# A decode kernel on one core: P V of loads 0 to 12 with 32 columns of P standing and V moving

## The chip, the core and the metric

The kernel runs on one core of a Trainium2 chip. A core has a matrix engine (PE), a vector engine (DVE), a scalar engine (ACT), a general engine (POOL), a queue engine (SP) that here issues almost all transfers, and sixteen DMA engines that carry them. [...] The metric is device time in microseconds (us) of one launch, median over runs.

A matmul has a stationary operand, which is loaded into the array first (LDWEIGHTS, "PEld" in the profile), and a moving operand, which is streamed through it. "Column groups" are matmuls whose stationary operand has 32 columns: each uses one quarter of the array and writes 32 partitions of PSUM, and four of them can be in flight side by side.

## The reference

One decode step of a transformer block for eight sequences: attention over the last 2048 cached positions with 32 query heads in 8 groups of 4, then an MLP whose token-mixing half vanishes for a sequence of length one.

```python
h = x + _A_ref(_layernorm(x), k_cache, v_cache, wq, wo)
out = h + _B_ref(_layernorm(h), w1, w2, w3, w4)
# _A_ref: B, D = 8, 512; Hq, Hkv, Dh = 32, 8, 128; W = 2048
q = (x @ wq) split into heads
scores = einsum("bhqd,bhkd->bhqk", q, k[last W]) * Dh**-0.5
p = softmax(scores); o = einsum("bhqk,bhkd->bhqd", p, v[last W])
return o @ wo
# _B_ref for S = 1: x1 = x (the shifted branch is zero); x1 + gelu(layernorm(x1) @ w3) @ w4
```

The caches are bfloat16. Of each, 8 x 8 x 2048 x 128 values are read, 33.5 MB.

## The kernel before

**Loads.** The caches are read in sixteen loads of 2 MB each for K and V. Load n belongs to sequence b = n // 2 and to half t = n % 2 of the eight groups (J = 4 groups). A partition holds 64 consecutive positions of one group: 32 partitions per group, four groups side by side. `load_k`, `load_v` and `load_wo` only issue transfers on SP's queue, in program order; a load waits there until its buffer is free (four buffers for K, four for V). `load_v(n)` waits for the last P V of load n − 4. The last load of V is cut into four pieces. All of wo, w3 and w4 follow at the end, but for two pieces of wo that are issued during loads 5 and 9.

**Engines.** Every engine has a list of operations (`PE.op`, `AC.op`, `DV.op`, `PO.op`), written in the order of the emission loop at the end of the function; each engine runs its list strictly in order, and an operation waits for the semaphore counts named in it. So the position of a call in the loop sets where an engine may stall.

**K.** `turn_K(i)` turns a quarter of a load, read as 32-bit words, with eight float32 transposes by PE (L296), into one of two PSUM tiles; ACT evicts the lower half (L283), DVE the upper (L284). `pe_QK(m)` multiplies with column groups of 32: a stationary 32-column window of `qz`, in which the four query columns stand at a place that depends on half and chunk, so that scores land in the right PSUM rows (L311). One PSUM tile `S_ps` holds the scores of a whole sequence.

**Softmax.** `softmax_1` to `softmax_3` take the row maximum (DVE L321), turn it (PE L325), reduce and negate it (DVE L327, L332), turn it back (PE L336) and take the exponential with its sum (ACT L342). In the next load `softmax_spread` writes P four times wider, P times a 0/1 mask over the four groups, in four parts of 512 columns (DVE L355); `softmax_4` turns this tile with sixteen bfloat16 transposes (PE L364), evicted through the same `turn` helper; `softmax_5` spreads the reciprocal of the sums (PE L372, DVE L375, L381).

**P V.** `pe_PV(i)` handles a quarter of a load: sixteen chunks of 128 positions, each one matmul with the chunk of V standing (128 columns) and 16 columns of the turned P moving (L397). All 64 matmuls of a load add up in the 16 columns `oT_ps[:, 0:16]`. `scale` (DVE L407) multiplies with the reciprocals, `turn_o` (PE L417, DVE L422) brings the result into the layout for wo.

**Order.** In iteration n of the loop K of load n is turned and scored and P V of load n − 3 is done (n − 4 in the last two iterations). The quarters of P V stand between the pieces of the score and softmax work (`pvs(1)` to `pvs(4)`); `turn_os` catches up with the out-turns near the start of an iteration. After the loop come, in this order, the spread of the last sequence, P V of load 12, softmax_5 and softmax_4, P V of loads 13 to 15 with half of wo in between (`pe_wo`), the rest of wo, and the MLP (L559 to L619).

Of the kernel before, what the change touches and what calls it, by code (L numbers as in the profile page):

```python
# [6 lines left out]
dt = mybir.dt  # L7
# [35 lines left out]
QW = 12 + R + 28  # L43
# [33 lines left out]
def bass_sequential_preLN__sliding_block_cached__mixer_s_mlp__decode_kernel(  # L77
# [24 lines left out]
    with es:  # L102
# [15 lines left out]
        perm_p = sb([128, 128], dt.bfloat16, "perm_p")  # L118
# [35 lines left out]
        oK = sb([128, 2, J, R, R], dt.bfloat16, "oK")  # L154
        o2 = sb([128, G, R, B], dt.bfloat16, "o2")
# [34 lines left out]
        def dma(eng, dst, src, sem, *waits):  # L190
            def f(e):
# [25 lines left out]
        e_sel = DV.op(lambda e: e.tensor_reduce(sel_f[:, :].rearrange("p (j h) -> p j h", j=J),  # L217
                                                ident_f[:, :].rearrange("p (j u h) -> p j h u", j=J, u=U),
                                                AX.X, ALU.add), e_idf)
        e_mE = DV.op(lambda e: e.tensor_reduce(mE[:, :], ident_f[:, :].rearrange("p (e k) -> p e k", k=R),  # L220
# [44 lines left out]
        def fill_q(b):  # L265
            for c in range(2):
                at = 12 + 16 * c
# [34 lines left out]
        def pe_QK(m):  # L302
            n, v = divmod(m, 2)
            b, t = divmod(n, NU)
            lo = 12 - 8 * v - 4 * t
# [18 lines left out]
        def softmax_2(b):  # L324
            e_mT[b] = PE.op(lambda e: e.matmul(sm[0:1, MROW], mcol[:, :], ident_f[:, :], start=True, stop=True),  # L325
                            e_max[b], sm_read[0], e_idf)
            e = DV.op(lambda e: e.tensor_reduce(Mrow[:, :].rearrange("o (j h) -> o j h", j=J),  # L327
                                                sm[0:1, MROW].rearrange("o (j u h) -> o j h u", j=J, u=U),
                                                AX.X, ALU.max), e_mT[b])
            sm_read[0] = e  # L330
            m_bc = bass.AP(tensor=Mrow[:, :].tensor, offset=0, ap=[[H, 1], [8, J], [0, U], [1, 8]])
            e_neg[b] = DV.op(lambda e: e.tensor_scalar(negrow[:, :].rearrange("o (j u h) -> o j u h", j=J, u=U), m_bc,  # L332
# [13 lines left out]
        def softmax_spread(b, part):  # L346
            if part == 0:
# [3 lines left out]
            p = P_sb[:, w * part:w * part + w]  # L351
            p_bc = bass.AP(tensor=p.tensor, offset=p.offset, ap=[p.ap[0], [1, w], [0, J]])
            m = mJ[:, :]
            m_bc = bass.AP(tensor=m.tensor, offset=m.offset, ap=[m.ap[0], [0, w], [1, J]])
            e_Pz[b, part] = DV.op(lambda e: e.tensor_tensor(  # L355
                Pz[:, 0, J * w * part:J * w * (part + 1)].rearrange("p (x j) -> p x j", j=J), p_bc, m_bc, ALU.mult),
                e_exp[b], e_PT.get(b - 1), e_mJ)

        def softmax_4(b):
            s = b % 2  # L360

            def mm(e, ps, half):
                for c in range(8 * half, 8 * half + 8):
                    ins = e.matmul(ps[:, c * 128:(c + 1) * 128], Pz[:, 0, c * 128:(c + 1) * 128], perm_p[:, :],  # L364
                                   is_transpose=True)
                return ins
# [20 lines left out]

        def pe_PV(i):
            n, w = divmod(i, U)
            b, t = divmod(n, NU)  # L390
            dst = oT_ps[:, 0:16]

            def f(e):
                for c in range(16):
                    o = (8 * (w % 2) + c // 2) * 128 + 16 * (2 * (2 * (c % 2) + w // 2) + t)
                    mvg = pS[:, b % 2, o:o + 16]
                    ins = e.matmul(dst, vnat[:, n % NV, (16 * w + c) * DH:(16 * w + c + 1) * DH], mvg,  # L397
                                   start=(w == 0 and c == 0), stop=(w == U - 1 and c == 15),
                                   skip_group_check=True)
                return ins  # L400
            e_PV[i] = PE.op(f, V(n, w), *e_pS[b], e_sc.get(n - 1))

        def scale(n):
            b, t = divmod(n, NU)
            src = oT_ps[:, 0:16]
# [3 lines left out]
                            e_rL[b], e_PV[U * n + U - 1], e_scale.get(n - 2))  # L409
# [54 lines left out]
        def emit_PV(i):  # L464
            if i % U == 1 and i > U:
                turn_os(i // U)
                if i // U == NUN - 1:
                    pe_wo((0, 1, 2, 3), e_scale[NUN - NU], (sem_wo, 16 * len(WO_AT)))
            pe_PV(i)
            if i % U == U - 1:  # L470
                scale(i // U)
# [184 lines left out]
```

## Time and profile before

| | |
|---|---|
| median of three runs | 197.41 us (197.41 to 197.92) |
| the profiled execution | 197.34 us, span 196.0 us |
| busy, PE / PEld / DVE / ACT / POOL | 153.8 / 125.9 / 98.2 / 85.9 / 7.0 us |
| DMA | 79.52 MB, mean 406 GB/s |
| mean granted clock of PE | 0.872 |
| P V on PE (L397) | 1024 matmuls, 33.2 us busy |
| turn of K on PE (L296) | 512 transposes, 76.1 us busy |
| turn of P on PE (L364) | 128 transposes, 9.4 us busy |
| spread of P on DVE (L355) | 32 instructions, 21.6 us busy |

How to read it: the span runs from the first to the last instruction of the profiled execution. Busy times of different engines overlap, and matmuls overlap one another, so they don't add up to the span. An arrow names what an engine waited for; "issue" means that the profile shows nothing that it waited for. The granted clock is 1.0 or 0.5 at any moment; 0.872 is its mean. The slices of the page are a fortieth of the span each, 4.9 us. Instructions of an engine are themselves brought by DMA, in queues of their own (q8 and q14 on the page).

### The profile page before, as it was taken

The numbers are of one execution on the slowest core, as the hardware profiler recorded it, in microseconds if no ns is written. First come the engines' busy times: TensorE is split into PE (matmuls) and PEld (weight loads), VectorE is DVE, ScalarE is ACT, GpSimd is POOL, SyncE is SP. The second block draws the span as 40 slices with busy tenths as digits, with TensorE's granted clock in tenths as the row PEclk, the third lists the DMA queues.
The fourth block names the chain that finished last, engine by engine and source line by source line (L and its number), as shares of the span: only waits on it lengthen the run. The fifth ranks groups of instructions, "written<-read, shape, count | busy, mean of one in ns | idle before, by whom it ended". The sixth has DMA issues, their size and how long they took to land.

```text
span 196.0 us, 5301 instructions
## 1 busy us (share of the span) xinstructions
PE 153.8 (78%) x2415; PEld 125.9 (64%) x2415; DVE 98.2 (50%) x223; ACT 85.9 (44%) x100; POOL 7.0 (4%) x28
## 2 busy tenths in 40 slices
PE   0038985978989898989885789898989897888464
PEld 0037852765869577868773668586958585777453
DVE  5302444865484566548553384549455765620130
ACT  6001565764456374735471355535635482230030
POOL 4001001001000100010001000100000000000000
PEclk9999999999699999997999579969997999555555
DMA  6999999999999999999999999999999999999970
GB/s 229 461 408 431 425 431 431 421 428 425 423 420 422 431 425 428 423 425 428 419 427 421 431 428 425 428 425 428 425 428 421 423 421 428 407 405 407 406 285 24
DMA packets 7542, 79.52 MB, mean 406 GB/s; under 512 B 856, under 2 KB 864, under 8 KB 3424
## 3 DMA queue, kind: packets, MB, share of 16 engines
q1 hardware_dynamic: 7504, 79.18, 96.1%
q8 instruction: 19, 0.31, 0.6%
q14 instruction: 3, 0.02, 0.0%
q10 hardware_dynamic: 16, 0.01, 0.0%
HBM read 79.18 MB, written 0.01 MB: 404 GB/s over the span
## 4 chain that ended last, share of the span: by engine, by line
DMA 51%; PE 31%; DVE 10%; SPq 5%; issue 2%
DMA knat<-in_A_k_cache_dram 42%; PE kT_ps L296 21%; DMA knat<-in_B_w_dram 9%; SPq L192 5%; PE S_ps L311 5%; DVE kT_sb L284 5%; DVE Pz L355 2%; PE kT_ps L364 2%; DVE mcol L321 1%; PE oT_ps L397 1%; PE sm L325 1%; PE sm L336 1%; DVE Mrow L327 1%; PE S_ps L607 1%; DVE negrow L332 0%
## 5 line engine op out<-in xcount | busy, mean ns | idle before, releaser
L283 ACT ACTIVATE kT_sb<-kT_ps 128x1024 bf16<-128x1024 bf16 x64 | 63.8, 1024 | 47.2 <-PE kT_ps L296 46.5
L296 PE MATMUL kT_ps<-perm_k,knat 128*128 128x128 f32 x512 | 76.1, 306 | 3.4 <-DMA knat<-in_A_k_cache_dram 3.2
L296 PEld LDWEIGHTS kT_ps<-perm_k,knat 128*128 128x128 f32 x512 | 65.7, 159 | 9.1 <-issue 4.3
L284 DVE TENSOR_SCALAR kT_sb<-kT_ps 128x512 int32<-128x512 int32 x64 | 44.2, 690 | 35.0 <-PE kT_ps L296 34.8
L397 PEld LDWEIGHTS oT_ps<-pS,vnat 128*128 128x128 bf16 x1024 | 30.5, 98 | 6.4 <-issue 6.1
L397 PE MATMUL oT_ps<-pS,vnat 128*128 128x16 bf16 x1024 | 33.2, 171 | 1.3 <-DVE oK L407 1.3
L311 PE MATMUL S_ps<-kT_sb,qz 128*32 128x512 bf16 x256 | 20.0, 386 | 11.0 <-DVE kT_sb L284 10.6
L355 DVE TENSOR_TENSOR Pz<-P_sb,mJ 128x512 bf16<-128x512 bf16 x32 | 21.6, 684 | 0.0
L342 ACT ACTIVATE P_sb<-S_ps,negcol 128x512 bf16<-128x512 f32 x8 | 5.5, 688 | 24.9 <-DVE negcol L339 24.9
L283 ACT ACTIVATE pS<-kT_ps 128x1024 bf16<-128x1024 bf16 x8 | 8.2, 1024 | 15.8 <-PE kT_ps L364 15.8
L311 PEld LDWEIGHTS S_ps<-kT_sb,qz 128*32 128x32 bf16 x256 | 4.7, 94 | 15.8 <-ACT kT_sb L283 14.8
L284 DVE TENSOR_SCALAR pS<-kT_ps 128x512 int32<-128x512 int32 x8 | 5.5, 692 | 9.4 <-PE kT_ps L364 9.4
L364 PEld LDWEIGHTS kT_ps<-perm_p,Pz 128*128 128x128 bf16 x128 | 8.1, 105 | 3.0 <-issue 3.0
L250 PE MATMUL S_ps<-xlnT,wbig 128*128 128x8 bf16 x128 | 3.6, 168 | 7.7 <-DMA wbig<-in_A_wq_dram 7.7
L364 PE MATMUL kT_ps<-perm_p,Pz 128*128 128x128 bf16 x128 | 9.4, 231 | 0.0
L407 DVE TENSOR_TENSOR oK<-oT_ps,rLk 128x64 bf16<-128x64 f32 x16 | 3.6, 224 | 11.1 <-PE oT_ps L397 11.1
L268 POOL COPY qz<-q_sb 64x64 bf16<-64x64 bf16 x16 | 4.6, 290 | 119.7 <-PE S_ps L311 103.5
L321 DVE TENSOR_REDUCE mcol<-S_ps 128x1 f32<-128x512 f32 x8 | 5.5, 692 | 6.5 <-PE S_ps L311 6.5
L250 PEld LDWEIGHTS S_ps<-xlnT,wbig 128*128 128x128 bf16 x128 | 3.5, 104 | 7.7 <-issue 7.7
L584 ACT ACTIVATE Pz<-oT_ps,eps 128x8 f32<-128x8 f32 x1 | 0.3, 268 | 15.0 <-PE oT_ps L583 15.0
L458 PE MATMUL S_ps<-o,wbig 128*128 128x8 bf16 x128 | 4.0, 168 | 2.3 <-issue 2.0
L255 DVE TENSOR_SCALAR kT_sb<-S_ps 128x256 bf16<-128x256 f32 x1 | 0.4, 425 | 10.0 <-PE S_ps L250 10.0
(83 smaller groups left out, 73.3 us busy)
## 6 DMA issues: line engine op xcount, KB each, us to landing
knat<-in_A_k_cache_dram SPq DMA_DIRECT2D x16, 2048.0 KB, 28.9
vnat<-in_A_v_cache_dram SPq DMA_DIRECT2D x15, 2048.0 KB, 30.8
wbig<-in_A_wq_dram SPq DMA_DIRECT2D x1, 4096.0 KB, 12.2
wbig<-in_A_wo_dram SPq DMA_DIRECT2D x2, 1024.0 KB, 30.8
vnat<-in_A_v_cache_dram SPq DMA_DIRECT2D x4, 512.0 KB, 9.4
wbig<-in_A_wo_dram SPq DMA_DIRECT2D x4, 512.0 KB, 11.8
knat<-in_B_w_dram SPq DMA_DIRECT2D x4, 448.0 KB, 13.0
knat<-in_B_w_dram SPq DMA_DIRECT2D x3, 512.0 KB, 16.6
```

Source lines behind the costliest of these rows:

```text
L192: e.dma_start(dst, src).then_inc(sem, 16)
L250: ins = e.matmul(S_ps[0][:, h * B:(h + 1) * B], wq_v[:, kc, h * DH:(h + 1) * DH], xlnT[:, kc * B:(kc + 1) * B], start=(kc == 0), stop=(kc ...
L268: e_qw[b] = PO.op(lambda e, c=c, at=at: e.tensor_copy(qz[64 * c:64 * (c + 1), b % 2, :, :, at:at + R], q_sb[64 * c:64 * (c + 1), :, :, b]. ...
L283: e_lo.append(AC.op(lambda e: e.activation(dst[:, 0:1024], ps[:, 0:1024], ACT.Copy), e_Tlo[k], *free))
L284: e_hi.append(DV.op(lambda e: e.tensor_single_scalar(dst[:, 1024:2048].bitcast(dt.int32), ps[:, 1024:2048].bitcast(dt.int32), 0, ALU.bitwi ...
L296: ins = e.matmul(ps[:, c * 128:(c + 1) * 128], src[:, c * 128:(c + 1) * 128], perm_k[:, :], is_transpose=True)
L311: ins = e.matmul(S_ps[b % 2][32 * j:32 * (j + 1), :].rearrange("p (c r) -> p c r", c=16), qz[:, b % 2, J * t + j, k, lo:lo + 32], kT[:, j, k],
L321: e_max[b] = DV.op(lambda e: e.tensor_reduce(mcol[:, :], S_ps[b % 2][:, :], AX.X, ALU.max), e_QK[4 * b + 3], e_mT.get(b - 1))
L342: e_exp[b] = AC.op(lambda e: e.activation(P_sb[:, :], S_ps[s][:, :], ACT.Exp, bias=negcol[:, s:s + 1], scale=1.0, accum_out=lcol[:, s:s + 1]),
L355: e_Pz[b, part] = DV.op(lambda e: e.tensor_tensor(Pz[:, 0, J * w * part:J * w * (part + 1)].rearrange("p (x j) -> p x j", j=J), p_bc, m_bc ...
L364: ins = e.matmul(ps[:, c * 128:(c + 1) * 128], Pz[:, 0, c * 128:(c + 1) * 128], perm_p[:, :], is_transpose=True)
L397: ins = e.matmul(dst, vnat[:, n % NV, (16 * w + c) * DH:(16 * w + c + 1) * DH], mvg, start=(w == 0 and c == 0), stop=(w == U - 1 and c == 15),
```

## The change

P V of loads 0 to 12 swaps its operands. The stationary operand is now 32 columns of P: the 16 columns of one chunk and the 16 of its neighbour. The moving operand is V of both chunks, 256 columns. Eight such matmuls do what sixteen did, four of them in different column groups, so that the sums stand in 4 x 32 rows and 256 columns of `oT_ps`. Half of these products (one chunk's P with the other chunk's V) is not used. Two halves of `oT_ps` are used in turn by even and odd loads.

What remains has to be added over the four column groups, and turned: `evict_o` copies the 128 x 256 float32 tile to SBUF on ACT, and `fold` multiplies it in two float32 matmuls with a 0/1 matrix `selo`, which picks the right rows for each half of the columns and gives the old 128 x 16 result in `sm[:, 32:48]`. The scaling on DVE moves into `fold` and reads that. The last three loads (13 to 15, `NST = 3`) keep the old form of P V (`f_last`), without eviction and fold.

For this the layout of P changes. Two chunks of P lie side by side as one 32-bit word: the spread writes 2 x 256 columns per part with a pair index innermost, and the turn of P is done on 32-bit words, with eight float32 transposes instead of sixteen bfloat16 ones. `perm_p` becomes float32, and the places of the query columns in `qz`, the order of the reduced maximum and of `sel_f` follow the new order of rows.

In the emission loop `fold_os` stands where `turn_os` stood, and `turn_os` comes after the first Q K of the iteration. In P V itself the fold of the load before stands ahead of a load's second quarter, and the out-turn ahead of its third.

```diff
-QW = 12 + R + 28
+QW = 24 + 32
+VP = 1
+MO = 32 * VP
+NO = 256 * VP
+TO = 128 // MO
+NST = 3
...
+        oE = sb([128, 512], dt.float32, "oE")
+        selo = sb([128, MO], dt.float32, "selo")
...
+        e_selo = DV.op(lambda e: e.tensor_reduce(selo[:, :], ident_f[:, :].rearrange("p (a x) -> p x a", a=TO),
+                                                 AX.X, ALU.add))
...
-            lo = 12 - 8 * v - 4 * t
+            lo = 24 - 16 * t - 8 * v
...
-            e_Pz[b, part] = DV.op(lambda e: e.tensor_tensor(
-                Pz[:, 0, J * w * part:J * w * (part + 1)].rearrange("p (x j) -> p x j", j=J), p_bc, m_bc, ALU.mult),
-                e_exp[b], e_PT.get(b - 1), e_mJ)
+            for a in range(w // 64):
+                o = w * part + 64 * a
+                p = P_sb[:, o:o + 64]
+                p_bc = bass.AP(tensor=p.tensor, offset=p.offset, ap=[p.ap[0], [1, RR], [0, J], [RR, 2]])
+                m = mJ[:, :]
+                m_bc = bass.AP(tensor=m.tensor, offset=m.offset, ap=[m.ap[0], [0, RR], [1, J], [0, 2]])
+                e_Pz[b, part] = DV.op(lambda e, o=o, p_bc=p_bc, m_bc=m_bc: e.tensor_tensor(
+                    Pz[:, 0, J * o:J * (o + 64)].rearrange("p (x j k) -> p x j k", j=J, k=2), p_bc, m_bc, ALU.mult),
+                    e_exp[b], e_PT.get(b - 1), e_mJ)
...
-                for c in range(8 * half, 8 * half + 8):
-                    ins = e.matmul(ps[:, c * 128:(c + 1) * 128], Pz[:, 0, c * 128:(c + 1) * 128], perm_p[:, :],
+                ps = ps[:, :].bitcast(dt.float32)
+                src = Pz[:, 0, :].bitcast(dt.float32)
+                for c in range(4 * half, 4 * half + 4):
+                    ins = e.matmul(ps[:, c * 128:(c + 1) * 128], src[:, c * 128:(c + 1) * 128], perm_p[:, :],
                                    is_transpose=True)
...
+            def f_last(e):
+                for c in range(16):
+                    cc = 8 * (w % 2) + c // 2
+                    o = 256 * (cc // 2) + 32 * (4 * t + 2 * (w // 2) + c % 2) + cc % 2
+                    ins = e.matmul(oT_ps[:, 0:16], vnat[:, n % NV, (16 * w + c) * DH:(16 * w + c + 1) * DH],
+                                   pS[:, b % 2, o:o + 31:2], start=(w == 0 and c == 0), stop=(w == U - 1 and c == 15),
+                                   skip_group_check=True)
+                return ins
             def f(e):
-                for c in range(16):
...
+                for c in range(8):
+                    cc = 8 * (w % 2) + c
+                    o = 256 * (cc // 2) + 32 * (4 * t + 2 * (w // 2)) + cc % 2
+                    q = c % TO
+                    ins = e.matmul(oT_ps[MO * q:MO * (q + 1), NO * (n % 2):NO * (n % 2 + 1)], pS[:, b % 2, o:o + 2 * MO - 1:2],
+                                   vnat[:, n % NV, (16 * w + 2 * c) * DH:(16 * w + 2 * c + 2) * DH],
+                                   start=(w == 0 and c < TO), stop=(w == U - 1 and c >= 8 - TO),
+                                   tile_position=(0, MO * q), skip_group_check=True)
+                return ins
+            e_PV[i] = PE.op(f if n < NUN - NST else f_last, V(n, w), *e_pS[b],
+                            e_ev_o.get(n - 1), e_sc[n - 1] if n > NUN - NST else None)
+
+        def evict_o(n):
+            e_ev_o[n] = AC.op(lambda e: e.activation(oE[:, NO * (n % 2):NO * (n % 2 + 1)], oT_ps[:, NO * (n % 2):NO * (n % 2 + 1)], ACT.Copy),
+                              e_PV[U * n + U - 1], e_fold.get(n - 2)) if n < NUN - NST else e_PV[U * n + U - 1]
+
+        def fold(n):
...
+            def f(e):
+                for s in range(2 * VP):
+                    o = NO * (n % 2) + 128 * s
+                    ins = e.matmul(sm[:, 32:48], oE[:, o:o + 128], selo[:, 16 * s:16 * s + 16],
+                                   start=(s == 0), stop=(s == 2 * VP - 1))
+                return ins
+            src = sm[:, 32:48] if n < NUN - NST else oT_ps[:, 0:16]
+            e_fold[n] = PE.op(f, e_ev_o[n], e_selo, sm_read[0]) if n < NUN - NST else e_ev_o[n]
...
         def emit_PV(i):
-            if i % U == 1 and i > U:
-                turn_os(i // U)
+            n, w = divmod(i, U)
+            if w == 1 and n <= NUN - NST:
+                fold_os(n)
+            if w == 2 or w == 1 and n > NUN - NST:
+                turn_os(n)
...
-            if i % U == U - 1:
-                scale(i // U)
+            if w == U - 1:
+                evict_o(n)
+                if n >= NUN - NST:
+                    fold_os(n + 1)
...
             turn_K(i)
             spread(0)
-            turn_os(pv[0] // U)
+            fold_os(pv[0] // U)
...
             pe_QK(2 * n)
+            turn_os(pv[0] // U)
```

## The prediction

> **What bounds the kernel now.** I read the page's slices first, then its queues, then two-microsecond windows and the order of time of the last 30 us.
>
> ```profile
> span 196.0 us, 5301 instructions
> PEclk9999999999699999997999579969997999555555
> DMA  6999999999999999999999999999999999999970
> q1 hardware_dynamic: 7504, 79.18, 96.1%
> q8 instruction: 19, 0.31, 0.6%
> ```
>
> The reader is to see that the DMA engines are busy in every slice up to the 38th, and that PE's granted clock is 0.5 in the last six. The groups of instructions, shapes apart, give the prices used below:
>
> ```profile
> L397 PE MATMUL oT_ps<-pS,vnat 128*128 128x16 bf16 x1024 | 33.2, 171 | 1.3 <-DVE oK L407 1.3
> L355 DVE TENSOR_TENSOR Pz<-P_sb,mJ 128x512 bf16<-128x512 bf16 x32 | 21.6, 684 | 0.0
> L342 ACT ACTIVATE P_sb<-S_ps,negcol 128x512 bf16<-128x512 f32 x8 | 5.5, 688 | 24.9 <-DVE negcol L339 24.9
> L372 PE MATMUL sm<-lsel,ones_f 128*128 128x32 f32 x16 | 3.5, 302 | 0.9 <-DVE o L422 0.9
> ```
>
> The mean of one is not its share of the path: matmuls overlap, so I price them by the distances between their starts. The order of time shows the end:
>
> ```profile
> 166.01 0.56 PE L397 MATMUL oT_ps<-pS,vnat 128*128 128x16 bf16 x16 [0.41 <-DVE oK L407]
> 166.31 2.49 DVE L355 TENSOR_TENSOR Pz<-P_sb,mJ 128x512 bf16<-128x512 bf16 x4
> 169.00 0.64 PE L372 MATMUL sm<-lsel,ones_f 128*128 128x32 f32 x2 [0.91 <-DVE o L422]
> 173.68 0.57 PE L397 MATMUL oT_ps<-pS,vnat 128*128 128x16 bf16 x16 [0.41 <-DVE oK L407]
> 182.00 0.65 PE L458 MATMUL S_ps<-o,wbig 128*128 128x8 bf16 x18 [0.33 <-DVE o L422]
> 184.35 1.39 PE L458 MATMUL S_ps<-o,wbig 128*128 128x8 bf16 x46 [1.70 <-issue]
> 188.54 1.28 ACT L597 ACT_TABLE_LOAD   x1
> 192.68 1.01 PE L607 MATMUL S_ps<-Pz,knat 128*128 128x8 bf16 x24 [0.16 <-DMA knat<-in_B_w_dram]
> ```
>
> At 192.68 PE still waits for the last weights, so DMA sets the end. It is not far ahead: PE went through attention until 181, and only the last landings hide that. Every 2 MB load ends with sixteen four-byte semaphore writes, one per DMA engine; in the packet records these lie 1.8 us apart at 22 us, 3.5 us at 164 us, and at the last load the first engine ends at 187.9, the last at 192.84. Each jump, by about 1.5 us, follows one of the 19 packets of the instruction queue (q8, 16 KB each, about 1.05 us), and they go round eight of the engines. So the last landing is that of an engine hit three times.
>
> **The change, part by part.** Sums go against the profiled execution: 197.34 us, which is its span of 196.0 and 1.34 around it; the median of the runs shown is 197.41.
>
> Set-up (one more reduction into selo, by L222's row 0.35 us; perm_p in float32, 0.25 by L229; a larger fill of qz, 1.27 x 1792/1408 = 1.6 us on POOL): nothing, because PE waits 7.7 us for wq meanwhile; without that cover 0.9 us. The new places of q and the reordered maximum row keep every shape: nothing, bounded by L327's 0.28 us a batch either way.
>
> P V (L397). Before, 64 matmuls per load start 25 to 27 ns apart at either clock: 1.65 us. After, 32 in column groups of four. The nearest row is Q K (L311): its four groups start 3 ns apart, the next four 213 ns later for 512 columns. With 256 columns that is 107 ns per four at full clock, 213 at half, so 0.85 us or 1.7 us a load, and 0.125 us where a full-array instruction follows (Q K: two times 213, next start after 0.55). Ends: 0.8 us (26 ns each) and 3.4 us (Q K unscaled). At half clock nothing is won.
>
> Fold, new on PE: two float32 matmuls, four passes. L372's passes start 132 ns apart at full clock and 235 at half: 0.53 or 0.94 us per load, thirteen times. Eviction, new on ACT: L342 takes 0.69 for 512 columns, L597 0.25 for 56, so 0.44 for 256. Behind it on ACT are the next K evictions (1.02 each); it stands where ACT idles before a load's first one, so 0 to 0.1 us.
>
> Turn of P: eight float32 turns. L296 starts them 109 ns apart (half clock 213), L364's sixteen 56 (107): 0.87 against 0.90. Nothing.
>
> Spread: eight instructions of 256 columns for four of 512. L355 issues every 0.60 us for 512 and L348's 32 columns take 0.15 (166.16 to 166.31), so 0.36 each: +0.12 us a part, +0.5 a batch on DVE (ends: 0.30, no fixed part, and 0.60). The scale of P V (0.2 us) moves from a gap into this DVE-bound stretch, the out-turn (0.14 on PE) behind Q K, without cost while Q K waits for evictions.
>
> No DMA changes. SP's loads of V wait for the last P V of a load; they are issued 15 to 27 us before an engine takes them, the last four (165.64) 2.5 us.
>
> Steady state, per batch: odd load +0.53 fold −0.15 last piece = +0.38; even load +0.68 on DVE −0.44 for three pieces in a row = +0.24. So +0.6 us a batch, 3.0 over the five batches from load 4 to 13. The cover is PE's wait for K at 106 to 109 (3.2 us) and at 148.22 (0.2): just enough, so it is hidden; without it the 3.0 us would be paid.
>
> The tail. K of load 14 lands at 148.2 in both. There the clock is 0.5 (149.2 to 152.6): the fold costs 0.94, of which 0.4 is left when the clock is back, and two more parts of the spread add 0.24: +0.65 at the turn of P. From there:
> - exp and its accumulator end at 166.8 (before 166.12). The eviction follows on ACT, and P V of load 12 waits for it: 167.3 (before 166.01).
> - Fold of load 11: +0.94. Its scale is now queued on DVE behind eight spreads, until 170.05 (166.95 + 2.88 + 0.22); the out-turn on PE waits for that, and behind it half of P V. softmax_5 starts at 171.2 (before 169.00).
> - Turn of P 1.71 as before, fold of load 12 +0.94: P V of load 14 starts at 176.8 (before 173.68), +3.1.
> - From there both kernels do the same, in the old form: the last wo groups start at 185.1 (before 182.00) and end, at 27 ns each, at 187.0.
>
> Instruction fetch. 4872 instructions of PE in 19 packets are 256 each, and PE runs dry at numbers 4290 and 4546, exactly 256 apart: the stalls at 177.66 (0.44 us) and 182.48 (1.87), each ending 2.47 us after its packet starts. The change takes away 832 (P V) and 128 (turn) and adds 104: 4016. The boundaries then lie at 3778 and 3522. Counted back from the end (statistics and MLP are 234) the first is two matmuls before the end of wo. A packet that starts as before, 37 to 157 instructions ahead, arrives between 186.5 and 188.6, against 186.9: +0.6 at the middle, and the boundary that now lies inside wo's first half adds 0.4 to the 0.44 of before. So wo ends at 188.0 (before 185.74). [...]
>
> After wo, from rows: 4.08 us to the end of the gelu table load (185.74 to 189.82), gelu 0.25, then 56 matmuls at 31 ns and the last one's flight: 6.3 us, so 194.3 against 193.69. The 2.33 us behind it stay: span 196.6, and with 1.34 **198.0**.
>
> What goes away: with 15 packets instead of 19, no DMA engine is hit three times; the last landing comes 1.4 us earlier (191.4). It is no longer what PE waits for.
>
> **Rivals.**
> 1. Fetch does not stall at the new boundary, for packets start early enough (157 ahead, as at 187.94). Then the 0.44 goes too, wo ends at 186.6, L607 at 192.9: span 195.2, **196.5**. For: fetch 18 caused no gap. Against: 16 and 17 did. It ends on the other side, faster; it decides when the packet starts before 184.0.
> 2. The tail runs at full clock. Then the turn of P takes 0.87, the two folds 0.53: −1.66 in all, PE is ready before the weights, and the landing decides: 197.34 − 1.4 = **195.9**. [...] Against: 0.5 from 166 to the end though PE is 55 to 100% busy in most windows there. [...]
> 3. PE falls behind K in the steady state, because a change between column groups and full-array work costs more than 0.125 us. It decides from 0.68 us a batch (3.4 of cover over five). With 0.06 more for each of the eight pieces a batch costs 1.1, and load 14 starts 5 x 1.1 − 3.4 = 2.1 late, less the 0.8 that the fetch stalls lose by a later start: **199.3**. For: the cover is thin. [...]
> 4. Nothing shows: DMA is 96.1% busy, and both the late tail and the earlier landing stay under it: **197.3**. [...]
>
> **How the numbers follow.** Forecast 0.42, rival 1 0.17, rival 2 0.12, rival 3 0.17, rival 4 0.12. This kernel's runs (197.41 to 197.92) tell 0.3%, 0.6 us, from no change. The forecast's own range is 197.4 to 199.0; with the rivals it is 196.1 to 199.4, which leaves out most of rival 2 and the far end of 3. Slower: forecast 0.36, rival 3 0.17, together 0.53. Within 0.3%: 0.06 of the forecast, 0.08 of rival 4 and 0.04 of rival 1, 0.18. Faster: 0.13 of rival 1, 0.12 of rival 2 and 0.04 of rival 4, 0.29.
>
> **What would show it.** P V in groups of four 107 or 213 ns apart; four float32 passes per load; ACT at 0.44; PE held before the out-turn of load 11 near 170; P V of load 14 near 176.8; a gap "issue" in the last matmuls of wo; the last weights landing near 191.4 with no PE wait at L607; 15 or 16 instruction packets. I am wrong if L607 still waits for DMA, or if load 14 does not start at the landing of K.

## The result and the profile after

The changed kernel takes 200.0 us (median; 198.7 to 202.5) against 197.41 of before (197.35 to 197.92), a ratio of 1.0106 with a 95% interval of 1.0074 to 1.0139: slower, by some three and a half times the 0.3% that was forecast. The ratios leave out executions more than 1.5% above the fastest of their kernel, here the two at 202.4; since the kernels with the new P V scatter more than before does, I give the median over all runs beside each ratio. The profiled execution took 199.77 us, with a span of 198.5 (before 197.34 and 196.0).

In the changed kernel's numbering L305 is the turn of K, L366 the spread, L377 the turn of P, L385 the matmul of softmax_5, L411 the old and L421 the new P V, L430 the eviction, L439 the fold, L445 the scale, L457 the out-turn, L462 its copy, L498 wo, L631 w3 and L659 w4; in the kernels below, added lines shift these by up to five (L416 in pad64 is the old P V, L633 in layout_best2 is w3). First the page of the changed kernel: span, clock and DMA in 40 slices, and two of the queues.

```profile
span 198.5 us, 4498 instructions
PEclk9999999999999999999998799999996999555555
DMA  6999999999999999999999999999999999999920
q1 hardware_dynamic: 7504, 79.18, 94.9%
q8 instruction: 15, 0.25, 0.5%
```

The share of DMA in the 39th slice is 0.2, where before had 0.7: the transfers end earlier, PE later. The instruction queue has 15 packets rather than 19, and the last landing of w4 is at 191.64 in the packet records (before 192.84). Both are as forecast. Next its groups of instructions (busy and mean of one, then idle time ahead of them and its main releaser):

```profile
L305 PE MATMUL kT_ps<-perm_k,knat 128*128 128x128 f32 x512 | 70.2, 290 | 2.0 <-DMA knat<-in_A_k_cache_dram 1.7
L366 DVE TENSOR_TENSOR Pz<-P_sb,mJ 128x256 bf16<-128x256 bf16 x64 | 23.8, 418 | 0.0
L421 PE MATMUL oT_ps<-vnat,pS 128*32 128x256 bf16 x416 | 20.6, 281 | 1.2 <-ACT oE L430 1.1
L385 PE MATMUL sm<-lsel,ones_f 128*128 128x32 f32 x16 | 3.5, 303 | 8.1 <-DVE o L462 8.1
```

The last line is new: PE waits 8.1 us in all ahead of softmax_5's matmul for the copy of the out-turn (before 0.9). Now the order of time at the end (start, duration, engine, line; in brackets the idle time ahead and its releaser):

```profile
154.70 0.41 PE L385 MATMUL sm<-lsel,ones_f 128*128 128x32 f32 x2 [1.10 <-DVE o L462]
157.44 1.09 PE L377 MATMUL kT_ps<-perm_p,Pz 128*128 128x128 f32 x8
...
167.39 0.37 ACT L430 ACTIVATE oE<-oT_ps 128x256 f32<-128x256 f32 x1
167.68 2.77 DVE L366 TENSOR_TENSOR Pz<-P_sb,mJ 128x256 bf16<-128x256 bf16 x8
167.91 0.40 PE L421 MATMUL oT_ps<-vnat,pS 128*32 128x256 bf16 x8 [1.09 <-ACT oE L430]
170.36 0.22 DVE L445 TENSOR_TENSOR oK<-sm,rLk 128x64 bf16<-128x64 f32 x1
170.63 0.20 PE L457 MATMUL sm<-oK,mE 128*32 128x16 bf16 x4 [1.44 <-DVE oK L445]
171.63 0.64 PE L385 MATMUL sm<-lsel,ones_f 128*128 128x32 f32 x2
177.32 0.57 PE L411 MATMUL oT_ps<-pS,vnat 128*128 128x16 bf16 x16 [0.52 <-DVE oK L445]
183.53 0.62 PE L498 MATMUL S_ps<-o,wbig 128*128 128x8 bf16 x17 [1.00 <-issue]
186.36 1.71 PE L498 MATMUL S_ps<-o,wbig 128*128 128x8 bf16 x58 [0.34 <-DVE o L462]
189.77 0.30 PE L498 MATMUL S_ps<-o,wbig 128*128 128x8 bf16 x6 [1.69 <-issue]
192.24 1.95 PE L631 MATMUL kT_ps<-Pz,knat 128*128 128x8 bf16 x56
194.47 1.65 PE L659 MATMUL S_ps<-Pz,knat 128*128 128x8 bf16 x56 [0.28 <-ACT Pz L649]
```

The chain is the forecast one: the eviction ahead of P V of load 12, the scale behind eight spreads, the out-turn waiting for it. The last wo groups start at 186.36 (before 182.00), 4.36 us late. Two lines say "issue" inside wo, with 1.00 and 1.69 us, where before had one of that size. Neither w3 nor w4 waits for DMA any more: PE now sets the end.

### The profile page after: what moved, and what is told of

The parts are those of the page before. It is cut to its first block, busy times and chain, and to the rows that moved or that the text cites. A ratio compares the mean times of both kernels' runs of the same rounds, so it can differ in the third digit from the quotient of the medians.

```text
span 198.5 us, 4498 instructions
## 1 busy us (share of the span) xinstructions
PE 145.5 (73%) x1987; PEld 112.6 (57%) x1987; DVE 101.2 (51%) x256; ACT 89.5 (45%) x113; POOL 7.4 (4%) x28
## 4 chain that ended last, share of the span: by engine, by line
DMA 40%; PE 36%; DVE 18%; issue 3%; ACT 1%; SPq 0%; DVEq 0%
DMA knat<-in_A_k_cache_dram 40%; PE kT_ps L305 17%; DVE kT_sb L293 7%; DVE Pz L366 6%; PE S_ps L320 4%; PE oT_ps L411 3%; PE kT_ps L377 2%; PE S_ps L498 2%; DVE mcol L330 1%; PE sm L439 1%; PE oT_ps L421 1%; PE sm L385 1%; PE S_ps L659 1%; PE sm L345 1%; PE sm L334 1%
## 5 line engine op out<-in xcount | busy, mean ns | idle before, releaser
L305 PE MATMUL kT_ps<-perm_k,knat 128*128 128x128 f32 x512 | 70.2, 290 | 2.0 <-DMA knat<-in_A_k_cache_dram 1.7
L305 PEld LDWEIGHTS kT_ps<-perm_k,knat 128*128 128x128 f32 x512 | 61.6, 152 | 8.7 <-issue 4.9
L366 DVE TENSOR_TENSOR Pz<-P_sb,mJ 128x256 bf16<-128x256 bf16 x64 | 23.8, 418 | 0.0
L421 PE MATMUL oT_ps<-vnat,pS 128*32 128x256 bf16 x416 | 20.6, 281 | 1.2 <-ACT oE L430 1.1
L421 PEld LDWEIGHTS oT_ps<-vnat,pS 128*32 128x32 bf16 x416 | 9.5, 97 | 6.2 <-issue 4.0
L377 PE MATMUL kT_ps<-perm_p,Pz 128*128 128x128 f32 x64 | 9.6, 298 | 0.0
L377 PEld LDWEIGHTS kT_ps<-perm_p,Pz 128*128 128x128 f32 x64 | 7.7, 154 | 3.0 <-issue 3.0
L385 PE MATMUL sm<-lsel,ones_f 128*128 128x32 f32 x16 | 3.5, 303 | 8.1 <-DVE o L462 8.1
L439 PEld LDWEIGHTS sm<-selo,oE 128*128 128x128 f32 x52 | 8.1, 223 | 1.1 <-ACT oE L430 0.9
L385 PEld LDWEIGHTS sm<-lsel,ones_f 128*128 128x128 f32 x16 | 2.6, 203 | 10.7 <-DVE o L462 9.8
L439 PE MATMUL sm<-selo,oE 128*128 128x16 f32 x52 | 8.4, 277 | 0.0
```

The lines of the kernel that those rows point to most:

```text
L305: ins = e.matmul(ps[:, c * 128:(c + 1) * 128], src[:, c * 128:(c + 1) * 128], perm_k[:, :], is_transpose=True)
L366: e_Pz[b, part] = DV.op(lambda e, o=o, p_bc=p_bc, m_bc=m_bc: e.tensor_tensor(Pz[:, 0, J * o:J * (o + 64)].rearrange("p (x j k) -> p x j k" ...
L377: ins = e.matmul(ps[:, c * 128:(c + 1) * 128], src[:, c * 128:(c + 1) * 128], perm_p[:, :], is_transpose=True)
L385: e_Lb[b] = PE.op(lambda e: e.matmul(sm[:, LB], ones_f[:, :], lsel[:, :], start=True, stop=True), e_lsel[b], sm_read[0])
L421: ins = e.matmul(oT_ps[MO * q:MO * (q + 1), NO * (n % 2):NO * (n % 2 + 1)], pS[:, b % 2, o:o + 2 * MO - 1:2], vnat[:, n % NV, (16 * w + 2 ...
L439: ins = e.matmul(sm[:, 32:48], oE[:, o:o + 128], selo[:, 16 * s:16 * s + 16], start=(s == 0), stop=(s == 2 * VP - 1))
```

## The experiments

All ratios are against the kernel before, on the same chip.

### The layout alone

```diff
-NST = 3
+NST = 16
```

> The new layout of P (spread with two chunks side by side, eight turns per row) with the old P V in all 16 loads: no eviction, no fold. Theory (the loss of the change lies in the tail, in the evictions, folds and scales behind the loop and in the stalls for instructions in the wo stage, and the steady state is paid by PE's waits for K): what is left is the P turn of the load-14 stage, 0.9 to 1.4 us later than the 156.11 of before (the longer spread, and softmax_5 waiting for a copy behind the spread), and the fetch boundaries: with 64 turns fewer than before they lie some 262 and 518 instructions before the end, so PE stops twice in the wo stage. P V of load 14 starts at 174.6 to 175.4, time 198.0 to 199.3. Rival 1 (the loss lies in the P V of the loads inside the loop): as before within 0.5, 197.0 to 197.9. Rival 2 (the layout is the whole loss): 199.5 to 200.5.

197.31 us (197.09 to 197.61), ratio 0.9981 (0.9967 to 0.9995): rival 1. The spread in eight pieces, the 32-bit turns and the new places of q cost nothing that arrives at the end. My theory had made the P turn too late (156.26, expected 157.0 to 157.5), and the end wrong:

```profile
174.23 0.57 PE L411 MATMUL oT_ps<-pS,vnat 128*128 128x16 bf16 x16 [0.52 <-DVE oK L445]
180.68 1.43 PE L411 MATMUL oT_ps<-pS,vnat 128*128 128x16 bf16 x48 [0.80 <-issue]
188.73 1.98 PE L631 MATMUL kT_ps<-Pz,knat 128*128 128x8 bf16 x56 [1.50 <-DMA knat<-in_B_w_dram]
192.47 1.01 PE L659 MATMUL S_ps<-Pz,knat 128*128 128x8 bf16 x24 [0.17 <-DMA knat<-in_B_w_dram]
```

PE is ready for w3 1.50 us before its weights are. The weights set the end, and a P V of load 14 that starts 0.55 us later than before's is hidden. So is the stop for instructions of 0.80 us ahead of the P V of load 15; the next boundary lies in w3, after that wait. The loss of the change comes with the new P V, then.

### The old P V already from load 11 on

```diff
-NST = 3
+NST = 5
```

> The change with the old P V from load 11 on instead of from load 13 on: loads 0 to 10 keep the new P V with its evictions and folds, and none of them is left behind the loop. Theory (loss in the tail): the P V of load 12 no longer waits for an eviction (0.5 us) and the out-turn of load 11 no longer for a scale behind the last spread (1.4 us), so the P V of load 14 starts at 175.3 to 175.9 rather than 177.32, and the time is 197.7 to 198.7. Rival (each new P V in the loop costs time that arrives at the end): 2 of 13 loads fewer, at most 0.4 us, 199.3 to 200.2.

Ratio 0.999 (0.9969 to 1.0012), but a median over all runs of 198.83 and times from 196.19 to 201.64, where before's runs lie within 1.3 us. The profiled execution took 197.76, and P V of load 14 started at 176.11, a little later than expected:

```profile
156.97 1.97 PE L377 MATMUL kT_ps<-perm_p,Pz 128*128 128x128 f32 x8
171.27 0.63 PE L385 MATMUL sm<-lsel,ones_f 128*128 128x32 f32 x2 [1.32 <-DVE o L462]
176.11 0.57 PE L411 MATMUL oT_ps<-pS,vnat 128*128 128x16 bf16 x16 [0.52 <-DVE oK L445]
```

Eleven loads keep the new P V, and the five executions in the ratio stand level with before. The other five took 199.8 to 201.6, as long as the change. The two groups differ in the mean clock (0.905 to 0.911, and 0.882 to 0.89). So the two loads whose evictions and folds lie at the tail hold between half of the loss, by the median of all runs, and the whole of it, by the ratio; this run does not decide it. The 1.97 us of the first line is the P turn at half clock (1.09 in the changed kernel's profile), of which more below.

### softmax_5 ahead of the out-turn

```diff
+            if t == 0 and b >= 1:
+                softmax_5(b - 1)
             turn_os(pv[0] // U)
-            if t == 0 and b >= 1:
-                softmax_5(b - 1)
```

> The change, with the matmul of softmax_5 put ahead of the out-turn in the loop, so that it no longer waits for the copy of the out-turn, which stands behind a part of the spread on DVE. The order behind the loop is left. Theory: the PE waits of 1.1 to 1.6 us ahead of that matmul vanish in all even loads; in loads up to 12 PE only waits longer for K, and in load 14 the P turn comes 0.6 to 0.9 us earlier than 157.44; P V of load 14 at 176.4 to 176.8, time 198.9 to 199.5. Rival 1 (the wait is paid in every even load): 7 waits of 1.2, less what K allows, 196 to 197.5. Rival 2 (the wait only moves to the out-turn or to the next matmul): 199.6 to 200.2.

1.0117 (1.0043 to 1.019), median over four runs 200.31: no gain, as in rival 2, 0.1 us above its range. In the profile (an execution of 202.28) the wait ahead of softmax_5 is gone, and the out-turn waits instead, for softmax_5's reciprocal, which stands behind the same part of the spread on DVE. In PE's order one of the two meets that queue.

### The out-turn earlier in the loop

```diff
+            turn_os(pv[0] // U)
             spread(2)
             pe_QK(2 * n)
-            turn_os(pv[0] // U)
```

> The change with the out-turn one place earlier in the loop, behind the third K turn and ahead of the third spread part and of the Q K products (the old place is ahead of the second K turn). Theory: its copy then stands ahead of the spread part on DVE, the matmul of softmax_5 finds it done, and the PE waits of 1.1 to 1.6 us ahead of that matmul go from every even load and come back nowhere. The P turn of the load-14 stage at 156.2 to 156.8 rather than 157.44; P V of load 14 at 176.1 to 176.8; time 198.6 to 199.5. Rival 1 (PE only waits elsewhere, for the scale or for the eviction by DVE): P turn at 157.3 to 157.6, 199.6 to 200.2. Rival 2 (the wait is paid in each even load): 197 or less.

Median 199.37, ratio 1.0086 (1.0052 to 1.0119): in the theory's range, but the gain of 0.2% on the change's 1.0106 is not separated by the intervals. The profile is the slowest of six executions, 200.41. The wait ahead of softmax_5 fell from 1.10 to 0.34 us in load 14, yet the P turn came at 158.80, later than the 157.44 of the changed kernel, and P V of load 14 at 178.18 (expected 176.1 to 176.8). The clock did that; the kernel nst3_best2 below has the same loop, and there the P turn is at 156.22. Two-microsecond windows of PE (length, busy, granted clock, DMA share, GB/s), first of turn_early, then of nst3_best2:

```profile
150.00:152.00 2.00, 2.00 (x12) 0.50 1.00 426
152.00:154.00 2.00, 2.00 (x11) 0.50 0.98 418
154.00:156.00 2.00, 1.72 (x18) 0.73 1.00 426
```

```profile
150.00:152.00 2.00, 2.00 (x20) 1.00 1.04 442
152.00:154.00 2.00, 1.26 (x19) 1.00 1.00 426
154.00:156.00 2.00, 1.12 (x16) 1.00 1.00 418
```

In the first two windows PE starts 23 matmuls at half clock and 39 at full clock. The clock had been the same in both up to 148.2; then turn_early had 0.5 for 6.8 us. The same instructions reach the P turn 2.58 us apart, which is as much as the whole loss of the change.

### More instructions at the start, to move the stops

The stops marked "issue" should belong to PE's instruction stream, in blocks of 256: in the changed kernel's trace they lie 502 and 246 instructions before the end, 256 apart. Small matmuls, put where PE waits for wq (136 in the first kernel, 64 in the second), push the block boundaries towards earlier work.

```diff
+        def pe_pad(e):
+            for _ in range(136):
+                ins = e.matmul(S_ps[1][:, 0:B], xln_b[:, 0:128], ident_b[0:B, 0:B], start=True, stop=True)
+            return ins
+        PE.op(pe_pad, e_xln, e_idb)
         e_q = PE.op(pe_q, e_xT, (sem_wq, 16))
```

> The change, with 136 small matmuls more at the start, while PE waits for wq (their result is overwritten). Theory (the stops of PE in the wo stage of 1.17 and 1.86 us come every 256 instructions of PE's own stream): the two stops leave their places, some 501 and 246 instructions before the end, for places 136 instructions earlier, in the P V of load 13 and in that of load 15, where an instruction takes longer and part of the fetch is hidden, and a third comes some 125 before the end, in w3 or ahead of w4; the wo groups run through, and the time is 197.2 to 199.2. Rival 1 (the stops belong to these matmuls, for instance to the arrival of wo): they stay where they are, 199.5 to 200.3. Rival 2 (a stop costs the same wherever it lies): they move, and the time stays within 0.4 of the changed kernel's.

> The change with 64 small matmuls at the start. A matmul is two instructions of PE (weights and product), so the 136 of the run before were 272 and moved the stops by 16 instructions only, from 501 and 246 to 517 and 262 before the end, which is what its trace shows. 64 are 128 instructions: the stops should now lie 630 and 374 instructions before the end, in the P V of load 14 and in that of load 15, and 118 before the end, at the border of w3 and w4. Theory (every 256 instructions PE stops for the next ones, and pays most where the 256 before were short): no stop inside the wo groups, the last wo ends 1.5 to 2.5 us earlier than 190.07, time 197.3 to 199.0. Rival (a stop costs the same in the P V, where a product takes 54 ns): the same time as the changed kernel, 199.3 to 200.3. Where PE's clock is granted at half in one more or one fewer stretch of 3.4 us, either moves by 1 to 2.

pad136 gave 1.0215 (1.0159 to 1.027), median 202.36, and shifted the stops by 16 instructions, from 502 and 246 before the end to 518 and 262, as 272 instructions modulo 256 must; why it is slower than the change by another 1% stays open (in its profile, of 200.57, 0.63 of the 0.80 us is there already at 165.7, ahead of the tail). pad64 gave 1.0085 (1.0068 to 1.0101), which the interval does not part from the change; the median, 199.08, lies between the theory's range and the rival's. What the theory said of the stops failed. The profile, of an execution of 203.13, shows one stop, where the boundary now lies, 374 instructions before the end, in the P V of load 15:

```profile
186.10 1.40 PE L416 MATMUL oT_ps<-pS,vnat 128*128 128x16 bf16 x47
190.33 0.19 PE L416 MATMUL oT_ps<-pS,vnat 128*128 128x16 bf16 x1 [2.83 <-issue]
```

One stop of 3.00 us from start to start replaces two of 1.17 and 1.86. So the stops do belong to blocks, and moving a boundary here only moved the waiting. (The products of P V there start 26 to 27 ns apart, as in wo, and not the 54 of the expectation.) What the traces share is the time from the first instruction of a block to the first of the next, wherever PE stood for about a microsecond or more at the boundary: before 6.25, the change 5.90 and 6.24, swap5 5.83 and 6.25, pad136 6.04 and 6.22, turn_early 5.69 and 6.24, nst3_best2 5.92 and 6.25, layout_only 5.56, layout_best2 5.87, tail_new 5.95, old_pv_from_11 and best 6.91, pad64 7.03, best_pad8 7.30. With stops under half a microsecond it was 5.73 (before), 5.29 (best) and 5.08 (old_pv_from_11). A block of wo is 128 products at 27 ns, 3.5 us of work.

### The tail put in order

A first try, best, has the out-turn early in the loop, the old P V from load 11 on, and softmax_5 after the first quarter of the P V of load 12; best_pad8 is the same with 8 padding matmuls.

```diff
-NST = 3
+NST = 5
...
+        emit_PVs(U * (NUN - 4) + 1)
+        softmax_5(NB - 1)
         emit_PVs(U * (NUN - 3))
-        softmax_5(NB - 1)
```

> The old P V from load 11 on, the out-turn early as in turn_early, and behind the loop the matmul of softmax_5 after the first quarter of the P V of load 12 rather than behind the out-turn of load 11. Theory: the end is the later of PE's tail and of the last landing of w4 plus 4.6 us (before: 192.84 and 197.41); here the last landing is that of the change less 0 to 0.2, 191.4 to 191.6, and PE's tail comes 1.5 to 3 us earlier than in old_pv_from_11 (P turn without the wait of 1.5 us, P V of load 14 at 173.8 to 174.8), so that the landing sets the end: 196.0 to 196.8, with little scatter. Rival (the P V of loads 0 to 10 makes PE late inside the loop, whatever the tail): 197.3 to 198.7.

> As best, with 8 small matmuls at the start, which put the stops for instructions 374 and 630 instructions before the end, into the P V of loads 15 and 14, rather than 358 and 614, the first of which is at the start of the last wo groups. Theory (the landing sets the end in best): no difference to best, 196.0 to 196.8. If PE still sets the end in best, this one is 0.8 to 1.8 us faster.

best: median 197.03, ratio 0.999 (0.9966 to 1.0015), P V of load 14 at 175.01, between theory and rival, since the out-turn of load 11 waited 2.31 us for softmax_5's reciprocal, again behind the spreads. best_pad8: 198.35, ratio 1.005 (1.003 to 1.0069), slower by 0.6%. Sixteen more instructions moved a boundary from the first wo matmuls of the last groups into the P V ahead of them, and its stop went from 1.92 to 3.27 us; both of its expected outcomes missed. In the two profiles 1.26 us of the later end are there already at P V of load 14, after a stretch at half clock that best did not have, and the other 1.0 comes with the stop.

Then four kernels with one order, the out-turn early in the loop and this behind it; they differ in NST, that is, in the old P V from load 13, 11, 0 or 15 on (in the last, the first wo groups follow the out-turn to the third quarter of load 15).

```diff
         for part in range(SPR):
             softmax_spread(NB - 1, part)
+            if part == 0:
+                fold_os(NUN - 4)
+                softmax_5(NB - 1)
...
         emit_PVs(U * (NUN - 3))
-        softmax_5(NB - 1)
         softmax_4(NB - 1)
```

> The common order, old P V from load 13 on as in the change. Theory: of the 2.6 us by which the change is slower, the order of the tail is 0.8 to 1.6; 198.0 to 199.0, P V of load 14 at 175.3 to 176.3. Rival (order is worth nothing, since the stops for instructions take up what is won): 199.2 to 200.2.

> The common order, old P V from load 11 on. Theory: the matmul of softmax_5 and the out-turn of load 11 no longer wait for spread parts 1 to 3 (2.7 us ahead of the out-turn in best); P V of load 14 at 173.8 to 174.6 rather than 175.01, 0.4 to 0.8 us faster than best: 196.1 to 196.8. Rival (the P turn waits for the spread anyway, so the wait only moves there): as best, 196.8 to 197.4.

> The common order, old P V in all loads. Theory (with the old P V throughout the last landing of the weights sets the end): PE's tail comes 0.5 to 1.2 us earlier than in layout_only and the time stays, 197.0 to 197.5; PE waits for the weights ahead of w3 and w4 for longer than there (1.86 and 0.77 us). Rival (PE sets the end there too): 196.0 to 196.6.

> First of four kernels with one common order, which differ in the loads that keep the old P V: here load 15 alone (the new P V in loads 0 to 14). The order: the out-turn early as in turn_early; behind the loop the scale of load 11 and softmax_5 directly after the first part of the last spread. Theory (PE's end is a chain of instruction blocks: from the crossing of one boundary of 256 instructions to the start of the next block it takes at least 5.6 to 7 us under DMA load, so that fewer instructions in the tail end it earlier): P V of loads 13 and 14 take 1.7 rather than 3.5 us each and 60 instructions less each, boundaries 126, 382 and 638 before the end; against that two more evictions and folds. 196.0 to 197.2. Rival (the evictions and folds of loads 12 to 14 cost more than the shorter P V saves): 198.0 to 199.5.

| kernel | old P V in loads | median, all runs | range | ratio, 95% |
|---|---|---|---|---|
| the change | 13 to 15 | 200.0 | 198.7 to 202.5 | 1.0106 (1.0074 to 1.0139) |
| nst3_best2 | 13 to 15 | 197.74 | 196.24 to 199.67 | 0.9993 (0.996 to 1.0026) |
| best2 | 11 to 15 | 196.97 | 195.98 to 197.46, and one of 239.71 | 0.996 (0.994 to 0.9981) |
| layout_best2 | all | 197.31 | 197.01 to 197.64 | 0.9985 (0.9971 to 0.9998) |
| tail_new | 15 | 198.16 | 195.88 to 200.61 | 0.9973 (0.9934 to 1.0013) |

nst3_best2 is the change with nothing but its order altered, and it wins the loss back, 1.1% (1.0106 against 0.9993), more than expected; by the medians over all runs 0.3 us of 2.6 are left. The clock alone does not explain it: at a mean clock of 0.89 to 0.90 its executions took 197.2 to 199.7, those of the change 200.0 to 202.5 at 0.885; at 0.91 to 0.92 they took 196.2 to 198.0, those of the change 198.7 and 199.8 at 0.906 and 0.91. Its tail, as the order of time shows it:

```profile
156.22 1.09 PE L377 MATMUL kT_ps<-perm_p,Pz 128*128 128x128 f32 x8
167.94 0.64 PE L385 MATMUL sm<-lsel,ones_f 128*128 128x32 f32 x2 [0.32 <-DVE oK L445]
169.34 0.23 PE L457 MATMUL sm<-oK,mE 128*32 128x16 bf16 x4
170.37 1.95 PE L377 MATMUL kT_ps<-perm_p,Pz 128*128 128x128 f32 x8
175.15 0.56 PE L411 MATMUL oT_ps<-pS,vnat 128*128 128x16 bf16 x16 [0.59 <-DVE oK L445]
187.60 0.30 PE L498 MATMUL S_ps<-o,wbig 128*128 128x8 bf16 x6 [1.71 <-issue]
```

P V of load 14 starts 2.17 us before the changed kernel's. Of these 1.22 are there at the P turn of load 14 (157.44 to 156.22), by the order in the loop and by the clock together (the changed kernel's was 0.5 from 149.0 to 152.4, this one's was full); the other 0.95 come behind the loop, where softmax_5 is now ahead of the out-turn and neither waits for the spreads (how much of the 0.95 is order and how much the clock, which was at half in other stretches there, no run separates). The stops remain, 1.71 us before the last six wo matmuls, neither w3 nor w4 waits for DMA, and the end moves with the tail: PE sets it.

layout_best2 is the counter-test. Its tail is 1.17 us earlier than layout_only's, and PE only waits longer for w3:

```profile
173.06 0.58 PE L411 MATMUL oT_ps<-pS,vnat 128*128 128x16 bf16 x16 [0.59 <-DVE oK L445]
189.03 1.98 PE L633 MATMUL kT_ps<-Pz,knat 128*128 128x8 bf16 x56 [2.55 <-DMA knat<-in_B_w_dram]
```

2.55 us against 1.50, and both at 197.31 us. With the old P V everywhere the landing of the weights sets the end, and what PE does earlier is lost.

best2 has the lowest median and beats both kernels: 0.4% under before (0.2 to 0.6%). Two executions at 195.98 lie below the theory's range, the median in the rival's, and the intervals do not part it from best. Its one profile fell into the execution of 239.71 us, with a mean clock of 0.58 (at 0.56 or 0.50 from 21.5 us on), so I show none.

tail_new gave 195.88 at best, the lowest here, and 200.61 at worst; its median lies in the rival's range, and four of ten executions, 195.88 to 196.94, in the theory's or just below it. P V of load 13 with all that stands in it took 2.49 us rather than 3.50, that of load 14 2.56 against 2.53: there the new form won nothing, though the clock was full. Its profile (196.94 us) shows why the low ones are low, in windows of PE:

```profile
169.00:172.50 3.50, 3.50 (x44) 0.55 0.96 382
172.50:175.50 3.00, 2.42 (x48) 0.96 1.02 412
175.50:179.00 3.50, 2.87 (x66) 1.00 1.03 412
```

From 172.8 to 179.6 the clock is full in a stretch where the changed kernel had 0.50. Over its ten executions the time follows the mean clock: 195.9 to 196.9 at 0.92 to 0.93, 198.1 to 198.6 at 0.905, 199.2 to 200.6 at 0.89 to 0.90.

## Why the prediction was right in its direction and wrong in its size

Right, with the measured number:

- Prices: the new P V issues in groups of four, 108 to 125 ns apart at full clock (forecast 107), the starts within most groups 1 to 6 ns apart, the eviction takes 0.37 (0.44), eight spreads 2.77 (8 x 0.36 = 2.88), and the set-up did not show.
- Steady state is covered: the turn of K of load 14 starts at 148.15 on the landing (148.2 forecast), after a wait for K of 1.05 us (the forecast left 0.4). Rival 3 did not happen.
- The last landing, 191.64 (191.4), and 15 packets; w4 does not wait for DMA. Rival 4 fell with that.
- After wo: 6.05 us to the end of w4's products (6.3), and 2.33 behind it.

Wrong, in the order of the sum:

- "two more parts of the spread add 0.24: +0.65 at the turn of P": it was +1.33 (157.44 against 156.11), with the clock at half in the same stretch of both profiles. First the lines of before, then the changed kernel's, whose next line is the wait of 1.10 us shown above:

```profile
152.82 0.61 PE L311 MATMUL S_ps<-kT_sb,qz 128*32 128x512 bf16 x8
153.37 0.41 PE L372 MATMUL sm<-lsel,ones_f 128*128 128x32 f32 x2
156.11 1.07 PE L364 MATMUL kT_ps<-perm_p,Pz 128*128 128x128 bf16 x16
```

```profile
152.97 0.62 PE L320 MATMUL S_ps<-kT_sb,qz 128*32 128x512 bf16 x8
153.41 0.19 PE L457 MATMUL sm<-oK,mE 128*32 128x16 bf16 x4
```

  At Q K the changed kernel is 0.15 us late (the forecast left 0.4 of the fold), at softmax_5's matmul 1.33. The step that said "the out-turn (0.14 on PE) behind Q K, without cost while Q K waits for evictions" overlooked its copy on DVE, which moved with it behind a spread part; softmax_5, next on PE, writes the tile that this copy reads (`sm`) and waited 1.10 us. From there to P V of load 14 the chain kept about 0.5 of the 0.68: exp's end 167.49 (166.8), P V of load 12 at 167.91 (167.3), out-turn 170.63, softmax_5 at 171.63 (171.2), P V of load 14 at 177.32 (176.8). turn_early cut the wait to 0.34 us.
- "Instruction fetch ... +0.6 at the middle, and the boundary that now lies inside wo's first half adds 0.4 to the 0.44 of before" is the term that failed. Both boundaries lay where the prediction put them (forecast two matmuls before the end of wo, found six before it), but PE stood for 1.17 and 1.86 us, start to start. Less the 0.03 from one product to the next, the stops were 1.14 (forecast 0.44 and 0.4, so 0.84) and 1.83 (forecast 0.6). From P V of load 14 to the end of wo 11.2 us were forecast and 12.75 measured: +1.55. The interval from packet to restart, 2.47, was right (2.54 and 2.64). The packets began 97 and 60 instructions ahead of their boundaries, inside the 37 to 157 of the forecast. What failed was to take the middle of that range for short work: 60 instructions of wo at 27 ns a pair are 0.8 us, and 2.64 less 0.8 are the 1.83. (The late end of the range was also short: 37 instructions are 0.5 us, and 186.9 − 0.5 + 2.47 is 188.9, not 188.6.) In the change the start went by time more than by count: in its last eight blocks, of 5.9 to 15.2 us each, the packet begins 2.8 to 3.8 us after the first instruction of the block that PE is in, and 60 to 219 instructions ahead of the boundary. In before's own trace the packet begins between 1.7 and 5.6 us after it, so a fixed delay is not shown. With the 6.25 of before's own trace, from 178.10 to 184.35, the end of wo follows from the measured first stop as 183.5 + 6.2 + 0.3 = 190.0; it was 190.07. What sets the start stays open.

0.5 and 1.55, less 0.2 behind wo, are the 1.8 us by which 198.0 missed the profiled 199.77. Rival 1, which left the stop out, went the wrong way for the same reason. Rival 2's number (195.9) is reached by the fastest executions once the tail is in order: 195.88 in tail_new, 195.98 in best2. That is not its mechanism, a tail at full clock that the landing ends: in tail_new's profile (196.94) the clock is at 0.5 from 179.6 on, and neither w3 nor w4 waits for DMA.

## What to carry to other kernels

When a step on one engine is moved, write down the queue of every other engine that serves it in the new order, and look for who waits behind: here a 0.23 us copy behind a spread part held PE for over a microsecond. A kernel whose last landing sets the end hides a late PE, and a change that makes DMA finish sooner and PE later takes that cover away from both sides; here the last landing went from 192.84 to 191.64 and the start of the last wo groups from 182.00 to 186.36. Ask then for PE's chain to the end at the clock that the trace shows there (here 0.5, in before from 166.25 us on and in the change from 169.44). In a tail of short matmuls like this one, with the DMA engines busy (a share of 1.03 from 179 to 184 us in the change), price each 256 PE instructions at the block time that the trace shows (here 5.56 us in layout_only to 7.03 in pad64 where PE stood for 0.8 us or more), not at the work alone.

## What the runs showed of the hardware

- In the tail PE stood at the ends of blocks of 256 instructions. At the three stops of over a microsecond in the traces of before (1.86 us) and of the change (1.17 and 1.86), the next block's packet began 3.79, 3.36 and 3.60 us after the block's first instruction and PE went on 2.47, 2.54 and 2.64 us behind that: 6.25, 5.90 and 6.24 us for 256 instructions of wo or P V, of which wo's work takes 3.5 (128 products at 27 ns). Moving the boundaries gained nothing clear of the noise (pad64, 1.0085 against the change's 1.0106; best_pad8, 1.005 against best's 0.999).
- After an instruction packet the last writes of a load lie further apart. In before all sixteen come within 0.56 us until the first packet (19.07); behind it one of them is late and they span 1.77, and behind the second (35.95) two are late. In the change the sixteen lie 2.1 us apart before the ninth packet (128.82) and 3.1 us after it, as if packets went round eight engines; the records of the packets name no engine, so this is inferred. The last landing is at 192.84 with 19 packets in before and at 191.64 with 15 in the change. In layout_only and layout_best2, where PE still waits for the last part of w4, it goes on at 192.47 and 192.78, close to before's 192.68.
- The granted clock was at 0.5 for 3.41 us (before at 50.2, 87.7, 128.7 and 149.2; the change at 108.0 and 149.0) or 6.83 (before at 108.2), and from 166.25 us (before) or 169.44 (the change) to the end. Within each of the two traces these stretches begin whole multiples of 3.41 us apart. Ahead of a fall PE had been busy for 0.32 to 0.87 of the 3.41 us by its records in before, and for 0.51 to 0.59 in the change; the clock stayed up after others at 0.51 (before from 29.7, the change from 29.5), and in the tail it stayed at 0.5 after 3.41 us with PE busy throughout (before from 169.7, the change from 172.9). What decides is open. One profile has a third value: 0.56, in best2's execution of 239.71 us, whose mean clock is 0.583. The stretches differ between executions of one kernel (before's mean clock lies between 0.851 and 0.886 over 31 executions), and one of 6.8 us in load 14 cost PE 2.6 us (turn_early against nst3_best2). Where the landing of the weights sets the end this doesn't show (layout_only: 0.5 us between its fastest and slowest run). Where PE does, the time went with the mean clock in tail_new (195.88 at 0.930, 200.61 at 0.888) and old_pv_from_11 (196.19 at 0.911, 201.64 at 0.882), but hardly in best (196.7 at 0.885, 198.4 at 0.903).
